# A retention layer and a gated feed-forward block on one core: next keys and queries prepared inside the group, activation table loaded early, w_in sums shared by VectorE and GpSimd

## The chip, the core and the metric

One core of a Trainium2 chip runs the whole kernel. The metric is the device time of one launch in microseconds. The kernel before takes 698.4 us (median of 3 runs, 698.11 to 699.78). q, k, v and the result are float32; the two weight matrices arrive as float64 and are made float32 in the kernel.

## The reference

A retention recurrence over 768 steps for 4 batches and 8 heads of 64 gives x, 3072 tokens of 512 features. A feed-forward block with 2048 hidden features follows, with the activation h * erf(softplus(h)).

```python
for t in range(S):
    state = gamma * state + einsum('bhd,bhe->bhde', k[:, :, t], v[:, :, t])
    y[:, :, t] = scale * einsum('bhd,bhde->bhe', q[:, :, t], state)
x = y.transpose(0, 2, 1, 3).reshape(3072, 512)
h = x @ w_in                       # w_in 512 x 2048
g = h * erf(softplus(h))
out = g @ w_out                    # w_out 2048 x 512
```

## The kernel before, in words

**Work items.** The recurrence is computed in 24 chunks j of 128 steps (6 for each batch). Each needs scaled keys and queries, their transposes, scores, a causal mask, products with the values, and an update of the state. The result lands transposed in xT, 512 tokens to a tile. The feed-forward block has a first stage and a second stage.

**First stage (g = 0 to 3).** The first 512 tokens go through plain matmuls. Group g covers 512 hidden features: `hidden` (L849 to L877) makes h, `gate_softplus` and `gate_erf` (L811, L824) apply the functions on ScalarE, `gated` (L843) multiplies by h on VectorE, and `project` (L879 to L899) multiplies by w_out one group later. In the same time the weights are brought from the 64-bit form in which they are stored to float32 by `conversion` (L285 to L336: L313, L317, L322, L325, L331 on VectorE, L314 on ScalarE). The conversions are steps of a generator; `pace(n)` emits n more of them and `need(...)` emits steps until a piece is done. `waiting` holds calls that `pace_around` runs in its middle.

**Second stage (g = 4 to 23).** The other 2560 tokens go in pairs of groups: a pair is one block of 256 tokens, its even group (g - 4 even) takes one half s = 0 of the hidden features, its odd group the half s = 1. Each group's first layer is computed by a bilinear scheme with 26 block products instead of 32. It needs sums of blocks of x (`x_sums`, 18 additions of 128x128, L931, once a pair) and sums of blocks of w_in (`sums_in(s)`, L338 to L343: 30 additions of 128x256 for each s, once in the kernel, on GpSimd). `hidden_steps` (L940 to L967) runs the 26 products (the table STEPS, L100): two matmuls each into one of four PSUM banks, after which ScalarE writes (L963, L965) or VectorE adds (L961) the bank into one or two of eight blocks of h. A later product that uses the same bank is added to what is there, so it has to wait until the bank has been read. The second layer is one with 7 block products instead of 8: it needs sums S1 to S4 of blocks of g (`g_sums`, L986) and T1 to T4 of blocks of w_out (`sums`, L345, L350: four additions of 128x1024 for each s, once in the kernel). `project_part(g, p)` (L1004) does product p; products 4, 5, 6, 7 use T4, T1, T2, T3.

**Order in a group g of the second stage (L1169 to L1228).** The order on every engine is the order in which the program emits instructions; nothing reorders them. A group emits the 26 steps, with products 1, 2, 4 of group g-1 after steps 14, 18 and 24, and with the S sums of g-1. Then come softplus (L811), `sub_visit(j, g)` (L707: TensorE's part of chunk j, and the scores of chunk j+1), in odd groups `x_sums` for the next pair, then `K_(j + 2)` and `T(j + 2)`, that is the scales (L509, L516 twice) and the two 32x32 block transposes (L531 twice) of the keys and queries of chunk j+2 on VectorE, the transfers of chunk j+3, erf (L824), products 5, 6, 7, 3 of group g-1, and `gated(g)` (L843 twice). In the first four groups a step of `last_steps` (the T sums) comes after projections (L1215, L1217, L1222). In g = 4 the projections of g = 3 are done: projection 0 after step 14 (L1187), 1 to 3 at the end (L1214).

**Around the change.** `sums_in(0)` is emitted in g = 3 (L1127) after `block_scales` (L472, which makes the scale table kq_b), `sums_in(1)` at the start of g = 4 (L1173). The keys and queries of chunk 6 and the x sums are emitted between the projections of g = 2 (L1157, L1160), the scores of chunk 6 at the start of g = 4 (L1174).

Of the kernel before, what the change touches and what calls it, by code (L numbers as in the profile page):

```python
# [12 lines left out]
F32 = mybir.dt.float32  # L13
# [6 lines left out]
P = 128  # L20
# [116 lines left out]
def kernel(  # L137
# [197 lines left out]
                done.update((which, 2 * i + u) for u in (range(2) if part is None else (part,)))  # L335
            yield  # L336

    def sums_in(s):  # L338

        assert all(("hidden", 2 * FG + s * FG + u) in done for u in range(FG))  # L340
        assert ("in", n_ft - 1) in done
        for to, a, b, sign in W_SUMS:
            nc.gpsimd.tensor_tensor(w_in_sb[:, s, to], w_in_sb[:, s, a], w_in_sb[:, s, b], op=OP[sign])  # L343

    def sums(s):  # L345

        assert ("project", s) in done
        x = {name: w_out_sb[:, s, at] for name, at in OUT.items()}
        for to, a, b in (("T1", "12", "11"), ("T2", "22", "T1"), ("T3", "22", "12"), ("T4", "21", "T2")):
            nc.vector.tensor_tensor(x[to], x[a], x[b], op=ALU.subtract)  # L350
            yield
        done.add(("sums out", s))

    done = set()

    def weights():


        pending = [conversion(n) for n in range(n_p)]
        begun = 0  # L360
        for n, steps in enumerate(pending):
            for k, _ in enumerate(steps, start=begun):
                yield
                if n > 4 and n + 1 < n_p and k == 2:
                    next(pending[n + 1])
                    yield
            begun = int(n > 4)

    def later_sums():
        for s in range(2):  # L370
# [132 lines left out]
    def ret_scale(j, i=None):  # L503

        if j >= NJ:
            return
        scaled.add(j)
        if j >= NB:
            nc.vector.tensor_tensor(  # L509
                KQ[j][:, 0], KQ[j][:, 0],  # L510
                kq_s[:, j % NC, 0, :, None].to_broadcast([P, H, D]), op=ALU.mult,
            )
            for i, x in enumerate((KB[j], KQ[j][:, 1].rearrange("p h d -> p (h d)"))):
                x = x.rearrange("p (u a d) -> p u a d", u=HP, d=32)
                by = kq_b[:, j % NC, i, :, :, None].to_broadcast([P, HP, 4, 32])
                nc.vector.tensor_tensor(x, x, by, op=ALU.mult)  # L516
            return
        part = slice(i, i + 1) if i is not None else slice(2)
        x = KQ[j][:, part]
        by = kq_s[:, j % NC, part, :, None].to_broadcast([P, x.shape[1], H, D])  # L520
        nc.vector.tensor_tensor(x, x, by, op=ALU.mult)
        pace(-1.1)

    def ret_transpose(j, part=None):
        assert j in scaled
        if j >= NB:
            for name, store, x in (
                ("k", KT, KB[j]), ("q", QT, KQ[j][:, 1].rearrange("p h d -> p (h d)"))
            ):
                store[j] = ret.tile([P, HP, C], F32, name=name + "T")  # L530
                nc.vector.transpose(store[j].rearrange("p u t -> p (u t)"), x)  # L531
            return
# [12 lines left out]
        pace(1)  # L545

    def ret_scores(j, pool=None):
        pp = SC[j] = [ret_psum(pool) for _ in range(2)]
# [455 lines left out]
    def project_part(g, p, at=slice(None)):  # L1004
        m, s = chunk_of(g), (g - G0) % 2
        if s == 0 and m not in O:
            O[m] = {}
            started.clear()
        a, b = PRODUCTS[p]
        if b[0] == "T":  # L1010
            need("sums out", s)
        i, half = (3, 1) if p == 4 and g >= NG - 2 else HOME[p]
        if i not in O[m]:
            O[m][i] = ps_o.tile([P, 2, DH], F32, name=f"o{i}")
        for u in range(FG):
            nc.tensor.matmul(  # L1016
                O[m][i][:, half, at],
                G[g][a][:, u * P : (u + 1) * P],
                w_out_sb[:, s, OUT[b], u, at],
                start=i not in started,  # L1020
                stop=(s == 1 and u == FG - 1),
                skip_group_check=True,
            )
            started.add(i)
        pace(1.5)
# [62 lines left out]
    def next_scores():  # L1088
# [35 lines left out]
        ],  # L1124
        [
            ([(load, 6), (sub_results, 5)], []),
            ([(load, 7), (block_scales,), (sums_in, 0)], [(sub_sums, 5)]),  # L1127
            ([], []),
            ([], []),
        ],  # L1130
    ]

    for g in range(G0):
        for u in range(FG):

            if g and u == (2 if g == 1 else 0):
                waiting.append((gated, g - 1))
            hidden(g, u)
            run(after[g][u][0])
            if (g, u) == (1, 0):  # L1140
                room = 0.0
            waiting.extend(after[g][u][1])
        gate(g)
        if g:
            for tt in range(TT):
                project(g - 1, tt)
                if g == 1 and tt < 2:
                    waiting.append((K_, 5) if tt else (sub_states, 4))
                elif g == 2 and tt == 0:
                    sub_results(4)  # L1150
                    sub_begin(5, ps_h)
                    load_block_scales()
                    waiting.append((sub_states, 5))
                elif g == 2 and tt == 2:
                    waiting.append((sub_sums, 4))
                elif g == G0 - 1 and tt == 0:
                    waiting.extend([(K_, JPC + 2), (T, JPC + 2)])  # L1157
                elif g == G0 - 1 and tt == 1:
                    load(JPC + 4)
                    waiting.append((x_sums, G0))  # L1160

    for _ in weight_steps:
        assert False, "weight steps left"

    j = JPC + 2
    put = None
    for g in range(G0, NG):  # L1169
        first = g == G0  # L1170
        more = j < NJ
        if first:
            sums_in(1)  # L1173
            sub_begin(j)  # L1174
            sub_states(j)
        elif put is not None:
            put_part(put, 0)
        more_sums = iter(()) if first else g_sums(g - 1)
        next(more_sums, None)
        for n, _ in enumerate(hidden_steps(g), start=1):  # L1180
            if first:
                if n in (5, 9):
                    gated(g - 1, n // 9)
                elif n == 14:
                    K_(j + 1)
                    T(j + 1)
                    project(g - 1, 0)  # L1187
                continue
            if put is not None and n in (14, 16, 18):
                put_part(put, n // 2 - 6)  # L1190
            for _ in range({14: 2, 18: 2}.get(n, 0) if put is None else {18: 1, 20: 1, 24: 2}.get(n, 0)):
                next(more_sums)
            if n in (14, 18, 24):
                project_part(g - 1, {14: 1, 18: 2, 24: 4}[n])
        put = None
        for _ in more_sums:
            pass

        gate_softplus(g)
        if more:  # L1200
            sub_visit(j, g)
        if g + 1 < NG and (g - G0) % 2:
            x_sums(g + 1)
        if more:
            if j + 2 < NJ:
                K_(j + 2)
                T(j + 2)
            if j + 3 < NJ:
                load(j + 3)
            j += 1  # L1210
        if first:
            gate_erf(g)
            for tt in range(1, TT):
                project(g - 1, tt)  # L1214
                next(last_steps)  # L1215
            put_first()
            next(last_steps)  # L1217
        else:
            gate_erf(g)
            for p in (5, 6, 7, 3):  # L1220
                project_part(g - 1, p)
                next(last_steps, None)  # L1222
            if (g - G0) % 2 == 0:
                put = chunk_of(g - 1)
        if g == NG - 1:
            last_gated(g)
        else:
            gated(g)  # L1228

    g, m = NG - 1, chunk_of(NG - 1)  # L1230
    for p, step in ((1, 0), (7, None), (2, None), (6, 1), (5, 2)):
# [56 lines left out]
```

## Time and profile before

| what | value |
|---|---|
| time, median of 3 | 698.4 us |
| span of the profiled execution | 697.9 us, granted TensorE clock 0.985 |
| first stage, to about 127.6 us | TensorE, VectorE nearly full; ScalarE about half |
| second stage, two groups | 53.9 us in most pairs |
| VectorE in two groups (244 to 298 us) | 39.7 us busy |
| GpSimd, w_in sums L343 | 60 instructions, 57.0 us busy, 113.5 to 172 us |
| ScalarE, table loads at L811 | 24 of 1283 ns |

Engines are PE (TensorE), PEld (its weight loads), DVE (VectorE), ACT (ScalarE), POOL (GpSimd) and SP (the queue that issues transfers). A line of a timeline gives start, length, engine, line of the program, operation, output <- inputs with shapes and a count; a bracket gives the idle time before it and what ended it. Idle time of an engine matters only where another engine, in the end TensorE, waits for it.

### The profile page before, as it was taken

Reading aid. Unit: us, or ns where it says so; the run is one execution under the profiler, and the core shown is the slowest. Engines: PE = TensorE matmul, PEld = TensorE weight load, DVE = VectorE, ACT = ScalarE, POOL = GpSimd, SP = SyncE. Lnnn points to the kernel's source line nnn. Section 1 sums busy time; section 2 is a strip of 40 time slices with the busy share of each in tenths; the row PEclk is TensorE's granted clock in tenths of the full one; section 3 lists DMA queues with packets and bytes.
Section 4 is the critical chain, followed back from the end, with each engine's and each line's share of the span. In section 5 each row is a group of like instructions: output and inputs, shape, how many; then the busy total and the mean of one; then the engine's idle time right before and its main releaser. Section 6 shows DMA issues by size and latency. Waiting matters only on the chain.

```text
span 697.9 us, 15334 instructions
## 1 busy us (share of the span) xinstructions
PE 665.0 (95%) x6240; PEld 565.4 (81%) x6240; DVE 521.4 (75%) x1067; ACT 267.8 (38%) x374; POOL 63.7 (9%) x80
## 2 busy tenths in 40 slices
PE   8999999799969989989989998998998998999998
PEld 7744444566969989989989998998998998999996
DVE  5999999889776786776775776777777577467364
ACT  3476545133414254153252451541541532424531
POOL 1000006998000000000000000000000000000000
PEclk9999999999989999999999999999999999999999
DMA  9999853333111222222321231231231220000000
GB/s 185 233 246 231 223 145 59 61 61 88 43 35 30 63 45 43 68 44 41 70 41 38 33 79 29 47 76 32 44 77 35 37 57 0 2 32 1 0 31 31
DMA packets 156726, 47.70 MB, mean 68 GB/s; under 512 B 143088, under 2 KB 147568, under 8 KB 156656
## 3 DMA queue, kind: packets, MB, share of 16 engines
q1 hardware_dynamic: 156240, 46.72, 30.5%
q8 instruction: 49, 0.80, 0.5%
q14 instruction: 21, 0.17, 0.1%
q10 hardware_dynamic: 416, 0.01, 0.0%
HBM read 40.39 MB, written 6.29 MB: 67 GB/s over the span
## 4 chain that ended last, share of the span: by engine, by line
PE 63%; DVE 20%; SPq 5%; issue 4%; ACT 4%; DMA 3%; DVEq 0%; ACTq 0%
PE o L1016 27%; PE hp L949 20%; PE r L949 10%; SPq L187 5%; DVE xs L931 4%; DVE e L843 2%; PE o L890 2%; DMA kq<-in_k_dram 2%; ACT e L811 1%; DVE h L961 1%; DVE w_out_sb L317 1%; DVE kb L516 1%; DVE kq L516 1%; DVE w_out_sb L325 1%; PE r L730 1%
## 5 line engine op out<-in xcount | busy, mean ns | idle before, releaser
L949 PE MATMUL hp<-xs,w_in_sb 128*128 128x128 f32 x1040 | 151.1, 282 | 21.8 <-DVE h L961 21.1
L949 PEld LDWEIGHTS hp<-xs,w_in_sb 128*128 128x128 f32 x1040 | 139.4, 197 | 27.5 <-DVE h L961 23.2
L1016 PE MATMUL o<-w_out_sb,h 128*128 128x256 f32 (+1 forms) x648 | 143.8, 379 | 0.4 <-DVE r L1243 0.4
L961 DVE TENSOR_TENSOR h<-h,hp 128x256 f32<-128x256 f32 x200 | 82.5, 420 | 74.6 <-PE hp L949 71.0
L1016 PEld LDWEIGHTS o<-w_out_sb,h 128*128 128x128 f32 x648 | 120.5, 190 | 17.1 <-DVE r L1243 0.6
L1016 PE MATMUL o<-w_out_sb,e 128*128 128x256 f32 x480 | 113.8, 380 | 0.0
L1016 PEld LDWEIGHTS o<-w_out_sb,e 128*128 128x128 f32 x480 | 87.0, 191 | 9.8 <-DVE e L977 0.4
L811 ACT ACT_TABLE_LOAD x24 | 30.8, 1283 | 153.0 <-DVE h L961 152.9
L961 DVE TENSOR_TENSOR h<-h,r 128x256 f32<-128x256 f32 x160 | 61.4, 418 | 22.9 <-PE r L949 19.2
L949 PE MATMUL r<-xs,w_in_sb 128*128 128x128 f32 x480 | 70.8, 287 | 4.9 <-DVE am L629 4.9
L949 PEld LDWEIGHTS r<-xs,w_in_sb 128*128 128x128 f32 x480 | 64.0, 203 | 5.1 <-issue 5.1
L963 ACT COPY h<-hp 128x256 f32<-128x256 f32 x40 | 14.9, 373 | 128.8 <-PE hp L949 92.6
L343 POOL TENSOR_TENSOR w_in_sb<-w_in_sb 128x256 f32<-128x256 f32 x60 | 57.0, 973 | 1.9
L843 DVE TENSOR_TENSOR e<-h,e 128x1024 f32<-128x1024 f32 x42 | 50.1, 1235 | 9.3 <-ACT e L824 9.3
L854 PE MATMUL hp<-xT,w_in_sb 128*128 128x512 f32 (+2 forms) x144 | 56.5, 548 | 0.0
L949 PE MATMUL hp<-xT,w_in_sb 128*128 128x128 f32 x320 | 48.9, 275 | 0.0
L854 PEld LDWEIGHTS hp<-xT,w_in_sb 128*128 128x128 f32 x144 | 25.7, 190 | 27.0 <-issue 24.6
L949 PEld LDWEIGHTS hp<-xT,w_in_sb 128*128 128x128 f32 x320 | 43.8, 192 | 1.5 <-issue 0.5
L965 ACT ACTIVATE h<-hp 128x256 f32<-128x256 f32 x60 | 23.1, 384 | 55.8 <-PE hp L949 54.4
L811 ACT ACTIVATE e<-h 128x2048 f32<-128x2048 f32 x22 | 42.0, 1911 | 5.3 <-DVE h L961 5.0
L824 ACT ACTIVATE e<-e 128x2048 f32<-128x2048 f32 (+1 forms) x23 | 42.1, 1836 | 0.2
L949 PE MATMUL r<-xT,w_in_sb 128*128 128x128 f32 x240 | 33.3, 275 | 0.0
(151 smaller groups left out, 780.1 us busy)
## 6 DMA issues: line engine op xcount, KB each, us to landing
w_out_sb<-in_moe_w_out_dram SPq DMA_DIRECT2D x14, 512.0 KB, 5.5
kq<-in_k_dram SPq DMA_DIRECT2D x23, 256.0 KB, 4.1
v<-in_v_dram SPq DMA_DIRECT2D x23, 256.0 KB, 3.1
out_dram<-r SPq DMA_DIRECT2D x23, 256.0 KB, 2.7
kq<-in_q_dram SPq DMA_DIRECT2D x288, 16.0 KB, 1.8
kb<-in_k_dram SPq DMA_DIRECT2D x288, 16.0 KB, 1.7
w_in_sb<-in_moe_w_in_dram SPq DMA_DIRECT2D x8, 512.0 KB, 11.3
w_in_sb<-in_moe_w_in_dram SPq DMA_DIRECT2D x8, 256.0 KB, 8.1
```

What stands on the lines that cost most here:

```text
L187: nc.sync.dma_start(to[part, u * C : (u + 1) * C].rearrange("p (a d) -> p a d", d=32), src[2 * u + s, :, d * 32 : (d + 1) * 32].rearrange( ...
L343: nc.gpsimd.tensor_tensor(w_in_sb[:, s, to], w_in_sb[:, s, a], w_in_sb[:, s, b], op=OP[sign])
L811: nc.scalar.activation(E[g], HS[g], AF.Softplus)
L824: nc.scalar.activation(E[g][:, half], E[g][:, half], AF.Erf)
L843: nc.vector.tensor_tensor(E[g][:, half], HS[g][:, half], E[g][:, half], op=ALU.mult)
L854: nc.tensor.matmul(HP_[ft][:, t], w_in_of(ft, kk), XC[0][:, kk, t], start=(kk == 0), stop=(kk == n_k - 1),)
L931: nc.vector.tensor_tensor(of(to), of(a), of(b), op=OP[sign])
L949: nc.tensor.matmul(to[:, u, :], w_in_sb[:, s, w, u * P : (u + 1) * P], XS[m](x), start=first and u == 0, stop=True, skip_group_check=True,)
L961: nc.vector.tensor_tensor(h, h, of, op=ALU.add if plus else ALU.subtract)
L963: nc.scalar.copy(h, of)
L965: nc.scalar.activation(h, of, AF.Copy, scale=-1.0)
L1016: nc.tensor.matmul(O[m][i][:, half, at], G[g][a][:, u * P : (u + 1) * P], w_out_sb[:, s, OUT[b], u, at], start=i not in started, stop=(s = ...
```

## The change

These things are changed. The five VectorE operations on the keys and queries are made a generator, `prepared(j)`; from g = 6 on, even groups emit those of chunk j+1 between their steps (10, 14, 16, 18, 24) and those of chunk j+2 where they were, and odd groups emit none; g = 4 and g = 5 each emit those of chunk j+1 between their steps. A small softplus on a spare tile is emitted ahead of each group's softplus, so that the table is loaded before h is complete. The w_in sums go to VectorE for s = 0 (16 after the piece ("out", 5) of the weights, 4 before g = 4, 10 in its first ten steps), and to GpSimd (20) and VectorE (10, behind erf of g = 4) for s = 1; a small GpSimd copy that reads the last sum of s = 0 stands ahead of GpSimd's twenty. Projections 0 and 1 of g = 3 ("two plain second-layer steps") are emitted ahead of the steps of g = 4, with gating, keys and queries, x sums and scores in between. The T sums are emitted in another order (T4 before T3) and at other places: two after the gating of g = 4, then after steps 1, 3 and 22 of g = 5 and 12 and 22 of g = 6, and the last one at the end of g = 6. The block scales are emitted two steps later.

The diff, cut to its core (the removed branches of `ret_scale` and `ret_transpose` for later chunks are the body of `prepared`):

```diff
-    def sums_in(s):
+    in_sums = [0, 0]
+    def sum_in(s, upto, engine=None):
-        for to, a, b, sign in W_SUMS:
-            nc.gpsimd.tensor_tensor(w_in_sb[:, s, to], w_in_sb[:, s, a], w_in_sb[:, s, b], op=OP[sign])
+        for to, a, b, sign in W_SUMS[in_sums[s] : upto]:
+            (engine or nc.vector).tensor_tensor(
+                w_in_sb[:, s, to], w_in_sb[:, s, a], w_in_sb[:, s, b], op=OP[sign]
+            )
+        in_sums[s] = max(in_sums[s], upto)
...
-        for to, a, b in (("T1", "12", "11"), ("T2", "22", "T1"), ("T3", "22", "12"), ("T4", "21", "T2")):
+        for to, a, b in (("T1", "12", "11"), ("T2", "22", "T1"), ("T4", "21", "T2"), ("T3", "22", "12")):
...
+            if pieces[n] == ("out", 5):
+                for k in range(4, 17, 4):
+                    sum_in(0, k)
+                    yield
...
+    def prepared(j):
+        if j >= NJ:
+            return
+        nc.vector.tensor_tensor(
+            KQ[j][:, 0], KQ[j][:, 0],
+            kq_s[:, j % NC, 0, :, None].to_broadcast([P, H, D]), op=ALU.mult,
+        )
+        yield
+        blocks = (KB[j], KQ[j][:, 1].rearrange("p h d -> p (h d)"))
+        for i, x in enumerate(blocks):
+            x = x.rearrange("p (u a d) -> p u a d", u=HP, d=32)
+            by = kq_b[:, j % NC, i, :, :, None].to_broadcast([P, HP, 4, 32])
+            nc.vector.tensor_tensor(x, x, by, op=ALU.mult)
+            yield
+        for name, store, x in zip("kq", (KT, QT), blocks):
+            store[j] = ret.tile([P, HP, C], F32, name=name + "T")
+            nc.vector.transpose(store[j].rearrange("p u t -> p (u t)"), x)
+            yield
...
-            ([(load, 7), (block_scales,), (sums_in, 0)], [(sub_sums, 5)]),
+            ([(load, 7)], [(sub_sums, 5)]),
             ([], []),
-            ([], []),
+            ([], [(block_scales,)]),
...
-                elif g == G0 - 1 and tt == 0:
-                    waiting.extend([(K_, JPC + 2), (T, JPC + 2)])
-                elif g == G0 - 1 and tt == 1:
-                    load(JPC + 4)
-                    waiting.append((x_sums, G0))
...
     j = JPC + 2
+    gated(G0 - 1)
+    all_of(prepared(j))
+    load(JPC + 4)
+    project(G0 - 1, 0)
+    x_sums(G0)
+    sub_begin(j)
+    project(G0 - 1, 1)
+    sub_states(j)
+    sum_in(0, 20)
...
+        next_chunk = prepared(j + 1) if even or put is None else iter(())
+        if put is not None:
+            order = {18: (e_sums,), 20: (e_sums,), 24: (e_sums, e_sums)}
+        else:
+            order = {
+                10: (next_chunk,), 14: (next_chunk, e_sums), 16: (next_chunk, e_sums),
+                18: (next_chunk, e_sums), 20: (e_sums,), 24: (next_chunk,),
+            }
+        if g == G0 + 1:
+            order.update({1: (last_steps,), 3: (last_steps,), 22: (last_steps,)})
+        elif g == G0 + 2:
+            order.update({12: (last_steps,), 22: (last_steps,)})
         for n, _ in enumerate(hidden_steps(g), start=1):
             if first:
+                sum_in(0, min(20 + n, len(W_SUMS)))
+                if n == 10:
+                    nc.gpsimd.tensor_copy(idle[:, :1], w_in_sb[:, 0, W_SUMS[-1][0], :1])
+                    sum_in(1, 20, nc.gpsimd)
...
+            for steps in order.get(n, ()):
+                next(steps, None)
...
+        nc.scalar.activation(idle[:, 1:], idle[:, 1:], AF.Softplus)
         gate_softplus(g)
         if more:
             sub_visit(j, g)
-        if g + 1 < NG and (g - G0) % 2:
+        if g + 1 < NG and not even:
             x_sums(g + 1)
         if more:
-            if j + 2 < NJ:
-                K_(j + 2)
-                T(j + 2)
+            if even and not first:
+                all_of(prepared(j + 2))
...
         if first:
-            gate_erf(g)
-            for tt in range(1, TT):
+            sum_in(1, len(W_SUMS))
+            for tt in range(2, TT):
                 project(g - 1, tt)
-                next(last_steps)
             put_first()
-            next(last_steps)
         else:
+            if g == G0 + 2:
+                all_of(last_steps)
             for p in (5, 6, 7, 3):
                 project_part(g - 1, p)
-                next(last_steps, None)
...
+        if first:
+            for _ in range(2):
+                next(last_steps)
```

More of the change, by code (lines that the diff above doesn't have):

```diff
@@ L336, in conversion @@
             yield
-    def sums_in(s):
+    in_sums = [0, 0]
+    def sum_in(s, upto, engine=None):
         assert all(("hidden", 2 * FG + s * FG + u) in done for u in range(FG))
-        assert ("in", n_ft - 1) in done
-        for to, a, b, sign in W_SUMS:
-            nc.gpsimd.tensor_tensor(w_in_sb[:, s, to], w_in_sb[:, s, a], w_in_sb[:, s, b], op=OP[sign])
+        for to, a, b, sign in W_SUMS[in_sums[s] : upto]:
[3 more added lines that the diff above has]
+        in_sums[s] = max(in_sums[s], upto)
     def sums(s):
@@ L348, in sums @@
         x = {name: w_out_sb[:, s, at] for name, at in OUT.items()}
-        for to, a, b in (("T1", "12", "11"), ("T2", "22", "T1"), ("T3", "22", "12"), ("T4", "21", "T2")):
+        for to, a, b in (("T1", "12", "11"), ("T2", "22", "T1"), ("T4", "21", "T2"), ("T3", "22", "12")):
             nc.vector.tensor_tensor(x[to], x[a], x[b], op=ALU.subtract)
+            done.add((to, s))
             yield
-        done.add(("sums out", s))
     done = set()
@@ L507, in ret_scale @@
         scaled.add(j)
[L508 to L517, printed above, removed]
         part = slice(i, i + 1) if i is not None else slice(2)
@@ L525, in ret_transpose @@
         assert j in scaled
[L526 to L532, printed above, removed]
         for i, (name, store) in enumerate((("k", KT), ("q", QT))):
@@ L1010, in project_part @@
         if b[0] == "T":
-            need("sums out", s)
+            assert (b, s) in done
         i, half = (3, 1) if p == 4 and g >= NG - 2 else HOME[p]
@@ L1155, with all_of @@
                     waiting.append((sub_sums, 4))
-                elif g == G0 - 1 and tt == 0:
-                    waiting.extend([(K_, JPC + 2), (T, JPC + 2)])
-                elif g == G0 - 1 and tt == 1:
-                    load(JPC + 4)
-                    waiting.append((x_sums, G0))
-    for _ in weight_steps:
-        assert False, "weight steps left"
-    j = JPC + 2
+    def all_of(steps):
+        for _ in steps:
+            pass
+    all_of(weight_steps)
+    idle = const.tile([P, 2], F32, name="idle_scalar")
@@ L1168 @@
+    nc.gpsimd.memset(idle, 1.0)
+    j = JPC + 2
+    gated(G0 - 1)
[7 more added lines that the diff above has]
+    sum_in(0, 20)
     put = None
     for g in range(G0, NG):
-        first = g == G0
+        first, even = g == G0, (g - G0) % 2 == 0
         more = j < NJ
[L1172 to L1176, printed above, removed]
-            put_part(put, 0)
@@ L1178 @@
-        more_sums = iter(()) if first else g_sums(g - 1)
-        next(more_sums, None)
+        if put is not None:
+            put_part(put, 0)
+        e_sums = iter(()) if first else g_sums(g - 1)
+        next(e_sums, None)
+        next_chunk = prepared(j + 1) if even or put is None else iter(())
+        if put is not None:
+            order = {18: (e_sums,), 20: (e_sums,), 24: (e_sums, e_sums)}
[4 more added lines that the diff above has]
+            }
@@ L1180 @@
+        if g == G0 + 1:
+            order.update({1: (last_steps,), 3: (last_steps,), 22: (last_steps,)})
+        elif g == G0 + 2:
+            order.update({12: (last_steps,), 22: (last_steps,)})
         for n, _ in enumerate(hidden_steps(g), start=1):
             if first:
[L1182 to L1188, printed above, removed]
+                sum_in(0, min(20 + n, len(W_SUMS)))
+                if n == 10:
+                    nc.gpsimd.tensor_copy(idle[:, :1], w_in_sb[:, 0, W_SUMS[-1][0], :1])
+                    sum_in(1, 20, nc.gpsimd)
@@ L1189 @@
             if put is not None and n in (14, 16, 18):
                 put_part(put, n // 2 - 6)
-            for _ in range({14: 2, 18: 2}.get(n, 0) if put is None else {18: 1, 20: 1, 24: 2}.get(n, 0)):
-                next(more_sums)
-            if n in (14, 18, 24):
+            for steps in order.get(n, ()):
+                next(steps, None)
+            if not first and n in (14, 18, 24):
                 project_part(g - 1, {14: 1, 18: 2, 24: 4}[n])
         put = None
-        for _ in more_sums:
-            pass
+        all_of(e_sums)
@@ L1199 @@
+        all_of(next_chunk)
+        nc.scalar.activation(idle[:, 1:], idle[:, 1:], AF.Softplus)
         gate_softplus(g)
@@ L1210 @@
             j += 1
+        gate_erf(g)
         if first:
-            gate_erf(g)
-            for tt in range(1, TT):
+            sum_in(1, len(W_SUMS))
+            for tt in range(2, TT):
                 project(g - 1, tt)
-                next(last_steps)
             put_first()
-            next(last_steps)
         else:
-            gate_erf(g)
+            if g == G0 + 2:
+                all_of(last_steps)
             for p in (5, 6, 7, 3):
                 project_part(g - 1, p)
-                next(last_steps, None)
-            if (g - G0) % 2 == 0:
+            if even:
                 put = chunk_of(g - 1)
```

## The prediction

> **What bounds the kernel now.** I read the page's parts 1 and 4 first, then the waits, then each engine's timeline around every idle stretch of TensorE. Busy time, shares of the chain, and two lines of the waits (waiter, releaser, us in total, times, longest):
>
> ```profile
> PE 665.0 (95%) x6240; PEld 565.4 (81%) x6240; DVE 521.4 (75%) x1067; ACT 267.8 (38%) x374; POOL 63.7 (9%) x80
> ...
> PE 63%; DVE 20%; SPq 5%; issue 4%; ACT 4%; DMA 3%; DVEq 0%; ACTq 0%
> ...
> PE hp L949 <- DVE h L961: 21.1, 11, 5.4
> PE r L949 <- DVE am L629: 4.9, 1, 4.9
> ```
>
> TensorE is the bound, and from 15 us to 134 us and inside most groups its timeline has no gap. So the change can win only the gaps and what follows them. TensorE's timeline shows them in brackets (start, length, what ran, idle before):
>
> ```profile
> 134.75 2.05 PE L949 MATMUL r<-xs,w_in_sb 128*128 128x128 f32 x8 [4.95 <-DVE am L629]
> ...
> 201.44 2.08 PE L949 MATMUL hp<-xs,w_in_sb 128*128 128x128 f32 x8 [5.41 <-DVE h L961]
> ...
> 257.67 1.16 PE L949 MATMUL hp<-xs,w_in_sb 128*128 128x128 f32 x8 [2.01 <-DVE h L961]
> ...
> 584.72 2.06 PE L949 MATMUL hp<-xs,w_in_sb 128*128 128x128 f32 x8 [2.00 <-DVE h L961]
> ```
>
> Seven stand at the ninth step of g=8, 10, ..., 20: 2.01, 1.81, 2.01, 2.01, 1.80, 2.01, 2.00, sum 13.65 us. Step 9 writes a PSUM bank that step 5 filled, so it waits until VectorE has read step 5. VectorE's timeline just before the gap of g=10 says why that read is late:
>
> ```profile
> 301.70 1.10 DVE L931 TENSOR_TENSOR xs<-xT 128x128 f32<-128x128 f32 x5
> ...
> 305.84 0.69 DVE L509 TENSOR_TENSOR kq<-kq,kq_s 128x512 f32<-128x512 f32 x1
> ...
> 308.86 2.32 DVE L843 TENSOR_TENSOR e<-h,e 128x1024 f32<-128x1024 f32 x2
> 311.10 0.42 DVE L961 TENSOR_TENSOR h<-h,hp 128x256 f32<-128x256 f32 x1
> ```
>
> The odd group ends with 18 x-sums (4.1 us), five operations on the next keys and queries (305.84 to 308.86, 3.0 us) and the gating (2.2 us). TensorE began g=10 at 306.03 and had the fifth step ready about 2.5 us later; the read came at 311.10.
>
> A gap also costs afterwards: the eight matmuls after 201.44 and 584.72 take 2.08 and 2.06 us instead of 1.16, as the granted clock falls (0.79 in 196 to 212 us). The distance between such gaps is 53.9 us, but 55.74, 55.75 and 56.23 where the clock fell: 1.86 us for a 2 us gap (3 of 7) and 2.3 us for the 5.4 us gap.
>
> **What the Trainium skill says.** "SBUF — State Buffer", section "SBUF: two separate sides": VectorE with two SBUF inputs and GpSimd reading SBUF exclude each other for a whole instruction. The trace agrees. While GpSimd does the w_in sums (113.5 to 172 us) the same operation takes 1.21 us that later takes 0.69, with no loss where an input is in PSUM (0.42 both times):
>
> ```profile
> 144.19 1.21 DVE L516 TENSOR_TENSOR kb<-kb,kq_b 128x512 f32<-128x512 f32 x1
> ...
> 306.44 0.69 DVE L516 TENSOR_TENSOR kb<-kb,kq_b 128x512 f32<-128x512 f32 x1
> ```
>
> "TensorE: Matmul & The Clock Gate", section "What's actually happening": the clock is halved after an idle window of some 3.4 us, and the window runs freely. That fits a cost of about 1.9 us which strikes only some 2 us gaps.
>
> **The change part by part.**
>
> *Keys and queries.* Odd groups lose the five operations. The gating of g=9 then ends at 311.1 - 3.0 = 308.1 or earlier, 0.4 us before step 5 of g=10 is ready: the gap closes. g=22, which has no keys left, already has none. The five go into even groups after steps 10, 14, 16, 18 and 24. I laid them between the reads of L961 with 0.60 us (scales), 0.63 (transposes), 0.33 (reads), from TensorE's start: a step is 0.446 us and a projection 1.73. The closest places are step 15, which needs the read of step 13 (done 7.1, needed 8.0), step 23 (12.6 against 13.3) and step 25 (14.9 against 15.9). All hold, so this adds nothing. Chunk j+2 stays at the end of even groups, where the read of step 5 had 1.28 us of slack (idle before 282.62). The transfers were issued two groups back. Gain: 13.65 + 3 x 1.86 = 19.2 us.
>
> *Table loaded early.* The 1.28 us load (L811, x24) follows 8 us of ScalarE idleness at every group, so the load and the small activation are hidden, and softplus, x-sums and gating come 1.28 us earlier. With the gaps closed nobody waits for that: zero, and at most the 0.4 us that weights waited for L977 in the last group.
>
> *Start of the second stage (127.6 us to the start of g=6 at 192.3).* Sixteen w_in sums on VectorE at 107 us: 128x256 interpolated between 0.20 us (128x128) and 0.60 (128x512) is 0.33, with some 0.12 for a dependent one: 6.4 us. Weights converted afterwards end at 123.5, erf of g=3 at 123.9 (ScalarE's L314 is queued behind), gating 126.2. TensorE wants it at 127.6: hidden by 1.4 us. Keys to 129.2, x-sums at uncontended speed (4.1 instead of 11.3 us) to 133.3. TensorE meanwhile has projection 0, scores, projection 1 until 135.5: the 4.95 us gap closes. The last 14 sums of s=0 lie among the reads of g=4 and end at 141.4; extra waits in g=4 are about 3 us; scores and projections 2, 3 end at 159.0, against 164.4 before.
>
> But g=5 needs the s=1 sums. GpSimd starts 20 at 141.7, at 0.72 to 0.77 us (its quiet pace: 16 to 17 in 11.5 us from 122 to 134 us, and a median of 768 ns), plus waits for VectorE: until 158.9 (up to 161.2 at its mean of 973 ns). Behind it on VectorE are queued the ten last sums, gating of g=4 (2.3 us) and four w_out sums (4.7 us) ahead of step 5's read: 161.3, 163.6, 168.3. TensorE, at step 9 by 163.4, waits until 168.7: a new gap of 5.3 us, and the clock falls (2 us). Before, step 9 of g=5 began at 169.85. From there to g=6 it is 22.45 us: 193.2 instead of 192.3, a loss of 0.9 us.
>
> *w_out sums moved.* Three stood before the gating of g=5 and made the 5.41 us gap; that and its 2.33 us of clock go: 7.7 us gained. They come back in g=6. T2 delays step 15 by 0.25 us. T4, after step 22, ends about 15.9 us into the group while product 4 could start at 14.4: 1.5 us. T3 stands behind the five operations at the end of g=6: where TensorE would reach product 7 about 3.5 us after the projections' start (at 276.6 in the timing of g=8), T3 would end near 278.95: 2.35 us. Sum 4.1, and with 3 in 7 for each of two gaps 1.6 us of clock: 5.7 us lost.
>
> *Sum:* 19.2 - 0.9 + 7.7 - 5.7 = 20.3 us: 698.4 - 20.3 = 678.1 us.
>
> **Rivals.** (1) *The wait moves into the even groups.* For it: VectorE was at work 20 of 27 us there and now reads PSUM in small pieces between 0.6 us blocks. Against: the free places counted above. At 1 us for 8 groups, with the clock falling in three, 8 + 5.6 = 14 us less: 692. At half of that, 685. (2) *The start goes better:* GpSimd at 0.72 us with no waits, gap under 3.4 us without a fall of clock, no clock loss in g=6: 20.3 + 2 + 2 + 1.6 = 26: 672; with the last group's 0.4 and no extra waits, 669. (3) *Slower:* if sixteen sums on a VectorE busy 39.45 of 40 us in 60 to 100 us reach the path (6.4 us), GpSimd's end comes 5 us later, and every even group stalls by 2 us with the clock falling each time (9 x 3.9 = 35): 698.4 - 20.3 + 6 + 5 + 35 = 724; with a fall in three of nine only, 713. Against: the sums come after all that TensorE needs before 127.6.
>
> **How the numbers follow.** Forecast (671 to 685) 0.70, rival 1 (685 to 695) 0.16, rival 2 (under 671) 0.07, rival 3 0.05, about no change 0.02. The range runs from 670 to 689: below it half of rival 2, above it half of rival 1 and the rest. Its unknown costs are GpSimd's pace (2.3 us), clock falls (2 each, up to three) and sums on VectorE (0.33 to 0.45 us each, 2 us). Chances: faster 0.92, same 0.03, slower 0.05.
>
> **What would show it.** No gap at step 9 of g=8 to 20 and 52 us for two groups instead of 53.9; no rise of waits inside even groups; one gap of 4 to 6 us in g=5, released by VectorE's first read of h there; in g=6 gaps of about 1.5 and 2.4 us at products 4 and 7, released by the w_out sums; the granted clock near 0.99. Wrong if even groups take over 26.2 us, if TensorE idles before 127 us, or if GpSimd's sums take over 1 us each.

## The result, and the profile after

The changed kernel takes 676.23 us (median of four executions, 675.23 to 677.14); the kernel before took 698.41 us (four, 698.11 to 699.78). The ratio is 0.9678 [0.9656, 0.9701]: 22.2 us, or 3.2%, faster. The prediction was 678.1. Single executions differ by some microseconds and by their granted clock, and the two that were profiled lie on opposite sides of their medians (before 699.63 us, after 675.38), so that spans read from the profiles differ by 24.6 us, more than the medians do.

The page after, parts 1 and 4 (busy time of each engine; shares of the chain that ended last), and from the waits the two largest that TensorE still has and one of VectorE (waiter, releaser, us in total, times, longest):

```profile
PE 657.0 (98%) x6240; PEld 558.1 (83%) x6240; DVE 519.7 (77%) x1107; ACT 272.1 (40%) x394; POOL 23.0 (3%) x42
...
PE 90%; DVE 5%; SPq 2%; DMA 1%; issue 1%; ACT 1%; DVEq 0%; ACTq 0%
...
PE hp L960 <- DVE h L972: 6.1, 3, 3.9
DVE xT L797 <- ACT xT L795: 4.8, 18, 1.4
PE o L1027 <- DVE w_out_sb L354: 3.4, 2, 2.2
```

The wait for VectorE's reads of h fell from 21.1 us in 11 places to 6.1 in 3. A new wait, for the w_out sums at L354, has 3.4 us. VectorE's wait for ScalarE's copies of xT was 26.5 us in as many places before; the experiments show which edit shortened it. VectorE did as much work as before (519.7 against 521.4 us), but on the chain its share fell from 20% to 5%.

The profiled executions split the gain in two. Before, TensorE was busy 665.0 of 697.9 us; after, 657.0 of 673.3. So 16.6 us are idle time that went (32.9 to 16.3), and 8.0 us are the same 6240 matmuls run at a higher granted clock (0.985 to 0.997).

Where this lies is told by the busy time of each engine in four stretches. In each line the stretch and its length are followed by TensorE's busy time, then PEld, VectorE, ScalarE and GpSimd, then the granted clock, the DMA share and GB/s. The kernel before:

```profile
127.00:193.00 66.00, 58.33 (x577) 47.33 (x576) 53.64 (x102) 21.64 (x34) 43.94 (x49) 0.97 0.31 65
193.00:245.00 52.00, 46.59 (x541) 43.96 (x539) 37.41 (x72) 14.64 (x25) 0.00 (x0) 0.93 0.20 42
245.00:349.00 104.00, 100.18 (x981) 93.56 (x982) 76.84 (x178) 38.81 (x58) 0.00 (x0) 1.00 0.25 52
349.00:660.00 311.00, 301.12 (x3148) 281.09 (x3148) 216.21 (x504) 118.25 (x168) 0.00 (x0) 0.98 0.18 37
```

The kernel after, the same stretches:

```profile
127.00:193.00 66.00, 59.10 (x581) 47.81 (x580) 58.55 (x136) 22.39 (x37) 16.14 (x21) 0.97 0.31 64
193.00:245.00 52.00, 48.56 (x555) 44.76 (x554) 38.62 (x87) 19.91 (x30) 0.00 (x0) 1.00 0.24 50
245.00:349.00 104.00, 104.00 (x1124) 97.41 (x1123) 78.92 (x185) 41.32 (x64) 0.00 (x0) 1.00 0.26 53
349.00:660.00 311.00, 310.95 (x3144) 291.00 (x3144) 223.94 (x514) 122.61 (x185) 0.00 (x0) 1.00 0.18 38
```

From 245 to 660 us TensorE has no gap and full clock. Between 127 and 193 us, where the sums were redistributed, it idles about as long as before (7.7 us before, 6.9 after). These are all its gaps after 125 us until the last group, from TensorE's timeline (start, length, what ran; in brackets the idle time before and what ended it):

```profile
143.81 0.71 PE L960 MATMUL hp<-xs,w_in_sb 128*128 128x128 f32 x4 [1.74 <-DVE h L972]
149.40 0.71 PE L960 MATMUL hp<-xs,w_in_sb 128*128 128x128 f32 x4 [0.51 <-DVE h L972]
161.91 0.68 PE L960 MATMUL hp<-xs,w_in_sb 128*128 128x128 f32 x4 [0.73 <-ACT h L974]
167.79 1.16 PE L960 MATMUL hp<-xs,w_in_sb 128*128 128x128 f32 x8 [3.85 <-DVE h L972]
207.77 1.99 PE L1027 MATMUL o<-w_out_sb,e 128*128 128x256 f32 x8 [1.20 <-DVE w_out_sb L354]
218.48 3.72 PE L1027 MATMUL o<-w_out_sb,h 128*128 128x256 f32 x16 [2.15 <-DVE w_out_sb L354]
```

The first two lie in g=4, where the last sums of s=0 stand among the reads. The third, early in g=5, was there before (0.73 us too). The fourth is the gap in g=5, the last two are those in g=6.

VectorE's timeline at the start of g=10 is the stretch in which the kernel before was late. It is now the reverse:

```profile
298.32 2.35 DVE L854 TENSOR_TENSOR e<-h,e 128x1024 f32<-128x1024 f32 x2
302.30 0.42 DVE L972 TENSOR_TENSOR h<-h,hp 128x256 f32<-128x256 f32 x1 [1.62 <-PE hp L960]
304.50 0.68 DVE L542 TENSOR_TENSOR kq<-kq,kq_s 128x512 f32<-128x512 f32 x1
307.09 0.68 DVE L551 TENSOR_TENSOR kb<-kb,kq_b 128x512 f32<-128x512 f32 x1
```

VectorE has done the gating and waits 1.62 us for TensorE's fifth step; the key operations come later, between steps. Two groups take 51.8 us from gating to gating (298.32 to 350.13), where 53.9 was the distance of the gaps before.

### The profile page after: what moved, and what is told of

Read it like the earlier page. It is cut to its first block, busy times and chain, and to the rows that moved or that the text cites. A ratio compares the mean times of both kernels' runs of the same rounds, so it can differ in the third digit from the quotient of the medians.

```text
span 673.3 us, 15344 instructions
## 1 busy us (share of the span) xinstructions
PE 657.0 (98%) x6240; PEld 558.1 (83%) x6240; DVE 519.7 (77%) x1107; ACT 272.1 (40%) x394; POOL 23.0 (3%) x42
## 4 chain that ended last, share of the span: by engine, by line
PE 90%; DVE 5%; SPq 2%; DMA 1%; issue 1%; ACT 1%; DVEq 0%; ACTq 0%
PE o L1027 35%; PE hp L960 21%; PE r L960 11%; PE hp L865 8%; PE o L901 7%; SPq L187 2%; PE r L741 1%; PE hp L633 1%; DVE w_in_sb L344 1%; PE o L777 1%; DVE h L972 1%; DVE w_out_sb L354 1%; DMA kq<-in_k_dram 1%; PE r L562 1%; PE o L609 1%
## 5 line engine op out<-in xcount | busy, mean ns | idle before, releaser
L960 PE MATMUL hp<-xs,w_in_sb 128*128 128x128 f32 x1040 | 147.0, 277 | 7.0 <-DVE h L972 6.1
L960 PEld LDWEIGHTS hp<-xs,w_in_sb 128*128 128x128 f32 x1040 | 135.7, 193 | 11.3 <-DVE h L972 7.4
L972 DVE TENSOR_TENSOR h<-h,r 128x256 f32<-128x256 f32 x160 | 59.9, 415 | 21.6 <-PE r L960 20.5
L960 PE MATMUL r<-xs,w_in_sb 128*128 128x128 f32 x480 | 67.1, 276 | 0.0
L960 PEld LDWEIGHTS r<-xs,w_in_sb 128*128 128x128 f32 x480 | 60.3, 193 | 0.0
L865 PEld LDWEIGHTS hp<-xT,w_in_sb 128*128 128x128 f32 x144 | 25.8, 190 | 27.0 <-issue 24.6
L835 ACT ACT_TABLE_LOAD x24 | 30.8, 1283 | 0.4
L960 PEld LDWEIGHTS r<-xT,w_in_sb 128*128 128x128 f32 x240 | 30.0, 192 | 0.0
```

Source lines behind the costliest of these rows:

```text
L835: nc.scalar.activation(E[g][:, half], E[g][:, half], AF.Erf)
L865: nc.tensor.matmul(HP_[ft][:, t], w_in_of(ft, kk), XC[0][:, kk, t], start=(kk == 0), stop=(kk == n_k - 1),)
L960: nc.tensor.matmul(to[:, u, :], w_in_sb[:, s, w, u * P : (u + 1) * P], XS[m](x), start=first and u == 0, stop=True, skip_group_check=True,)
L972: nc.vector.tensor_tensor(h, h, of, op=ALU.add if plus else ALU.subtract)
```

## The experiments

The theory: the keys and queries at the ends of odd groups cost nearly all that the change gains, through the seven gaps and the clock; the new start only exchanges one gap for others; the early table is hidden. The rivals: the gain comes from the table or from the redistributed sums, or the key operations would make even groups wait.

### One edit at a time on the kernel before

**Keys alone.** From g=7 on, the five operations leave the ends of odd groups and go into even groups.

```diff
+        inside = not first and (g - G0) % 2 == 0
+        next_chunk = prepared(j + 1) if inside and g > G0 + 2 else iter(())
         for n, _ in enumerate(hidden_steps(g), start=1):
+            if n in (10, 14, 16, 18, 24):
+                next(next_chunk, None)
...
-            if j + 2 < NJ:
+            if j + 2 < NJ and (g == G0 + 1 or (g - G0) % 2 == 0):
                 K_(j + 2)
                 T(j + 2)
```

> The kernel before with one edit: from g = 7 on the keys and queries leave the odd groups and go between the steps of the even groups. Theory of the prediction: the seven 2 us gaps at step 9 of g = 8 to 20 and three falls of the clock go, 13.65 + 5.6 = 19.2 us, so 679 us; the 5.41 us gap of g = 6 stays. Rival (the work only moves the wait into the even groups): gaps of about 1 us inside g = 8, 10, ..., 20 and no more than 6 us gained, 692 us or above.

680.14 us (679.96 to 681.05) against 699.33 (seven executions): ratio 0.9718 [0.969, 0.9746]. That is 19.2 us (17.8 to 21.7 by the interval), the size of the term in the prediction. No gap is left from g=8 to the last group, and the gaps at the start of g=4 (5.22 us) and in g=6 stay. TensorE's timeline of this kernel:

```profile
201.86 2.07 PE L969 MATMUL hp<-xs,w_in_sb 128*128 128x128 f32 x8 [5.41 <-DVE h L981]
```

**Table alone.** One small softplus ahead of `gate_softplus` in the kernel before.

```diff
+    idle2 = const.tile([P, 1], F32, name="idle_scalar")
+    nc.gpsimd.memset(idle2, 1.0)
...
+        nc.scalar.activation(idle2, idle2, AF.Softplus)
         gate_softplus(g)
```

> The kernel before with one edit: the small softplus ahead of each softplus. Theory (one chain, softplus - x sums - keys - gating, makes the gap, so anything cut out of it shortens it): the seven gaps fall from 2.0 to 0.7 us and the one of g = 6 from 5.41 to 4.1, with no fall of the clock after the seven: 8 x 1.28 + 5.6 = 15.8 us, so 682.6 us. Rival (the load is hidden in ScalarE's idle time and is worth nothing by itself, as it was costed in the prediction): 698.4 us.

684.96 us (684.62 to 685.06): ratio 0.9785 [0.9752, 0.9818], 14.4 us. Each of the eight gaps lost 1.28 us, the length of the load. Two of them in TensorE's timeline:

```profile
201.04 1.73 PE L949 MATMUL hp<-xs,w_in_sb 128*128 128x128 f32 x8 [4.12 <-DVE h L961]
...
308.12 1.16 PE L949 MATMUL hp<-xs,w_in_sb 128*128 128x128 f32 x8 [0.52 <-DVE h L961]
```

What were gaps of 1.8 to 2.0 us at step 9 of g=8 to 20 are now 0.72, 0.52, 0.73, 0.72, 0.52, 0.72, 0.72 (sum 4.65 instead of 13.65), and the clock falls after none of them. So 9.0 us of gaps, 1.3 in g=6 and three falls of 1.86 us are in it: 15.9 us, which the interval (12.7 to 17.3) takes in. The load was on the chain that makes the gaps. VectorE's timeline ahead of g=10, in the kernel before and in this one:

```profile
301.10 0.56 DVE L786 TENSOR_TENSOR xT<-xT,hp 128x128 f32<-128x128 f32 x2 [1.43 <-ACT xT L784]
```

```profile
297.65 0.56 DVE L786 TENSOR_TENSOR xT<-xT,hp 128x128 f32<-128x128 f32 x2 [0.16 <-ACT xT L784]
```

ScalarE does the load, the softplus and then the copy of xT for which this addition waits; behind the addition VectorE has the x sums, the five key operations, the gating and the read of step 5, and step 9 waits for that read. In all, VectorE waits 26.5 us for these copies in the kernel before, with the keys alone and in the changed kernel without the early table, and 4.8 us wherever the table is early. The Trainium skill ("ScalarE: Activation LUTs", section "What ACT_TABLE_LOAD costs") gives about 1283 ns for the load, which the traces show, and 1380 ns of drain with it; the gaps shrink by the 1.28 us alone.

### One edit taken out of the changed kernel

**No early table:** the line with the small softplus goes.

```diff
-        nc.scalar.activation(idle[:, 1:], idle[:, 1:], AF.Softplus)
         gate_softplus(g)
```

> The changed kernel without the small softplus that loads the table early. Theory of the prediction: in pairs from g = 8 on nothing waits for the 1.28 us, so no gap comes back; only where the T3 sum is the last to arrive (product 7 of g = 6, now a gap of 2.15 us) and in the last group does it show: 1.3 + 0.4 us, so 677.9 us. Rival (the early load carries part of the gain): 1.28 us for each of nine pairs, 11.5 us, so 688 us.

679.21 us (678.49 to 679.66): ratio 0.9701 [0.9673, 0.973]. Only one gap changed, the last one in g=6, from 2.15 to 3.43 us. TensorE's timeline:

```profile
220.84 4.33 PE L1027 MATMUL o<-w_out_sb,h 128*128 128x256 f32 x11 [3.43 <-DVE w_out_sb L354]
```

VectorE's timeline shows where it comes from:

```profile
215.76 0.56 DVE L797 TENSOR_TENSOR xT<-xT,hp 128x128 f32<-128x128 f32 x2 [1.43 <-ACT xT L795]
...
219.60 1.18 DVE L354 TENSOR_TENSOR w_out_sb<-w_out_sb 128x1024 f32<-128x1024 f32 x1
```

The addition to xT waits 1.43 us for ScalarE again (0.16 in the changed kernel), and the five key operations and T3, the sum at 219.60, stand behind it. The gap is 1.28 us longer, with a lower clock afterwards (0.992 over the span instead of 0.997). Once the keys have moved, the table is worth these 1.28 us and the clock: about 3 us by the medians, though the two ratios' intervals overlap.

**Keys back:** from g=5 on the five operations stand at the ends of groups, and the table stays early.

```diff
-        next_chunk = prepared(j + 1) if even or put is None else iter(())
+        next_chunk = prepared(j + 1) if g < G0 + 2 else iter(())
...
-            if even and not first:
+            if not first:
                 all_of(prepared(j + 2))
```

> The changed kernel with the keys and queries back at the ends of all groups from g = 5 on, the early table load kept. Theory (the early load and the move of the keys shorten the same chain): gaps of about 0.7 us come back at step 9 of g = 8 to 20, and one of about 1.6 us in g = 6, no fall of the clock; the T4 gap of g = 6 (1.2 us) goes as VectorE is freer there: 676.2 + 5 + 0.2 = 681.5 us. Rival (the two edits are separate, the keys carry 19 us by themselves): 695 us.

684.2 us (682.84 to 685.75): ratio 0.9774 [0.9739, 0.9809]. Gaps of 0.53 to 0.72 us are back at step 9 of g=6, 8 to 20. Two expectations missed. The gap of step 9 in g=6 was to be about 1.6 us and is 0.72. The gap of product 4 in g=6 was to go with the key operations, and stayed at 1.12 us. T4 is emitted after step 22, so VectorE takes it only after the read of that step; its place, not VectorE's load, makes it late.

**The new start alone:** both of the above edits together, so that only the sums, the start of the second stage and the places of the w_out sums differ from before.

> The changed kernel with both steady edits undone: no early table load, and from g = 5 on keys and queries at the end of every group. What is left is the new start of the second stage (shared w_in sums, two projections ahead, w_out sums moved). Theory of the prediction (that part only exchanges gaps): seven gaps of 2 us with three falls of the clock, in g = 6 one of 2.0 at step 9, 1.1 at product 4 and 3.4 at product 7, 3.85 in g = 5: 676.2 + 19.2 + 2.0 + 1.3 = 698.7 us, the time of before. Rival (the start carries a part of its own, the 4.95 and 5.41 us gaps that it closes): 692 us or less.

700.68 us (twelve executions, 699.62 to 702.44) against 701.32 (fifteen): ratio 1.0005 [0.9991, 1.002]. TensorE's timeline of g=6:

```profile
198.82 1.16 PE L960 MATMUL hp<-xs,w_in_sb 128*128 128x128 f32 x8 [2.01 <-DVE h L972]
211.06 1.99 PE L1027 MATMUL o<-w_out_sb,e 128*128 128x256 f32 x8 [1.13 <-DVE w_out_sb L354]
223.06 3.72 PE L1027 MATMUL o<-w_out_sb,h 128*128 128x256 f32 x16 [3.44 <-DVE w_out_sb L354]
```

The one gap of 5.41 us has become three of 6.58 together. The 4.95 us at the start of g=4 are gone, but step 9 of g=5 waits 3.84 us (0.77 before) and g=4 has 2.3 us inside it (1.23 before). By itself this third of the change is worth nothing that can be measured.

| edits in the kernel | ratio to before |
|---|---|
| start and w_out sums | 1.0005 [0.9991, 1.002] |
| table | 0.9785 [0.9752, 0.9818] |
| keys | 0.9718 [0.969, 0.9746] |
| start, table | 0.9774 [0.9739, 0.9809] |
| start, keys | 0.9701 [0.9673, 0.973] |
| all three | 0.9678 [0.9656, 0.9701] |

The table and the keys shorten the same chain: 2.15% and 2.8% alone, but no more than 3.2% together with the start. Table and keys without the start were not run, so what the start adds beside both of them is not measured.

### The w_in sums of s=0 on GpSimd

All thirty go back to GpSimd, at the piece of the weights where VectorE did sixteen.

```diff
             if pieces[n] == ("out", 5):
-                for k in range(4, 17, 4):
-                    sum_in(0, k)
-                    yield
+                sum_in(0, 30, nc.gpsimd)
```

> The changed kernel with the 30 w_in sums of s = 0 all on GpSimd, emitted at the place where VectorE now starts them; the s = 1 sums are shared as in the changed kernel. Theory (the ports of VectorE and GpSimd exclude each other): the x sums take about 11 us again instead of 4.1 and end near 140, so TensorE has a gap of about 4.5 us at the start of g = 4 with a fall of the clock, but the stalls in g = 4 (1.74 and 0.51) go, and as GpSimd's twenty sums still start near 141 the gap of g = 5 shrinks by what the start lost: 676 to 678 us. Rival (sharing the sums carries several us of its own): 682 us or more.

678.65 us (676.02 to 680.38) against 700.09 (seven): ratio 0.9708 [0.9681, 0.9735], which overlaps that of the changed kernel. GpSimd began at 92.5 us and was at work, with one break of 2.4 us for other operations, until 153 us. The expectation missed in part: the x sums were to take about 11 us and TensorE to wait 4.5 us at the start of g=4. VectorE's timeline of this kernel:

```profile
129.58 1.21 DVE L540 TENSOR_TENSOR kq<-kq,kq_s 128x512 f32<-128x512 f32 x1
...
136.88 2.37 DVE L940 TENSOR_TENSOR xs<-xT,xs 128x128 f32<-128x128 f32 x3
...
158.82 4.14 DVE L344 TENSOR_TENSOR w_in_sb<-w_in_sb 128x256 f32<-128x256 f32 x10
```

Beside GpSimd a key operation takes 1.21 instead of 0.68 us and the x sums end 7.4 us after they began (4.1 in the changed kernel), so TensorE waits 2.67 us for the transposed queries at 134.4 us. On the other hand GpSimd is done earlier, VectorE's last ten sums run alone in 4.14 us instead of 6.55, and the gap in g=5 is 1.44 instead of 3.85. What is won at one end is paid at the other. For these thirty sums the choice of the engine made no difference that can be measured; the run moves their engine and their time together, so it can't tell the two apart.

### The gaps that the change leaves

**w_out sums earlier in g=5 and g=6.** T2 of s=1 to the end of g=5, T4 to step 12 of g=6 and T3 ahead of the key operations.

```diff
         elif g == G0 + 2:
-            order.update({12: (last_steps,), 22: (last_steps,)})
+            order.update({12: (last_steps,)})
...
             x_sums(g + 1)
+        if g in (G0 + 1, G0 + 2):
+            next(last_steps)
```

> The changed kernel with three w_out sums of s = 1 moved: T2 to the end of g = 5 behind the x sums (1.42 us of slack there), T4 to step 12 of g = 6, T3 ahead of the five key operations at the end of g = 6. Theory of the prediction (the two gaps of g = 6, 1.20 and 2.15 us, come only from where the sums stand in VectorE's order): both go and nothing comes back, 676.2 - 3.35 = 672.9 us. Rival (VectorE has no room, the gaps come back at step 9 of g = 6 or of g = 7): 676 us.

671.64 us (671.57 to 672.38) against 701.32: ratio 0.9586 [0.9566, 0.9607]. Both gaps in g=6 are gone; that in g=5 is 3.84 as before.

**And fewer of them ahead of step 5 in g=5.** The two that stood after steps 1 and 3 of g=5 go after steps 12 and 22, and the rest move on by the same number of places.

```diff
         if g == G0 + 1:
-            order.update({1: (last_steps,), 3: (last_steps,), 22: (last_steps,)})
+            order.update({12: (last_steps,), 22: (last_steps,)})
         elif g == G0 + 2:
-            order.update({12: (last_steps,)})
+            order.update({5: (last_steps,), 12: (last_steps,)})
```

> As the run before, and in g = 5 only two w_out sums (T1, T2) stand ahead of the first read of h, T4 goes behind step 12 and T3 behind step 22; in g = 6 T2 goes behind step 5. Theory (the gap of g = 5 is VectorE's queue: GpSimd's sums, the last ten sums, gating, four w_out sums): the gap of 3.85 us falls by 2 x 1.15 to 1.55 us and the clock does not fall behind it (1.8 us): 672.9 - 4.1 = 668.8 us. Rival (the gap is set by GpSimd's sums alone): 672.9 us.

668.16 us (667.86 to 668.42): ratio 0.9533 [0.9509, 0.9557]. TensorE's timeline in g=5:

```profile
165.89 1.16 PE L960 MATMUL hp<-xs,w_in_sb 128*128 128x128 f32 x8 [1.45 <-DVE h L972]
```

The two sums took 2.4 us ahead of the read and the gap shrank by 2.4; the clock is at 1.000 over the span, and the time fell by 3.5 us.

**GpSimd makes fourteen of the s=1 sums, VectorE sixteen,** four of them behind the mask of the scores in g=4.

```diff
             sub_mask(j + 1)
+        if g == G0:
+            sum_in(1, 18)
...
-                    sum_in(1, 20, nc.gpsimd)
+                    sum_in(1, 14, nc.gpsimd)
```

> As the run before, and GpSimd takes 14 of the sums of s = 1 instead of 20, VectorE 16, of which four stand behind the mask of chunk 7, where VectorE waits for ScalarE. Theory (VectorE waits for GpSimd's last sums, 6.55 us for ten sums that take 3.6 alone): GpSimd ends 4 us earlier, VectorE has 6 more sums of 0.36 us, 1.4 of them in idle time, so the gap of g = 5 falls by another 1 to 1.5 us: 667.5 us. Rival (one sum costs as much wherever it stands): 668.8 us.

667.49 us (667.23 to 667.65): ratio 0.9524 [0.9505, 0.9544], the best of all: 4.8% under the kernel before, where the changed kernel is 3.2% under. The gap in g=5 fell only from 1.45 to 1.15 us; 1 to 1.5 us less was expected. Six sums fewer on GpSimd are six more on VectorE, which has the reads and the gating of the same stretch to do. The step from the version before is within both intervals.

## Why the prediction was right, point by point

**Keys and queries: right.** 19.2 us were predicted; alone they brought 19.2, and all seven gaps went. That the two agree to a tenth is luck, as the interval is 17.8 to 21.7. The reason holds in detail: VectorE was to be ready 0.4 us before step 5 of g=10; with the keys alone it waits 0.34 us there, and 1.62, the table's 1.28 more, in the changed kernel. No read in an even group came too late: TensorE is busy 104.00 of 104 us from 245 to 349 us. Rival 1 is out.

**The table: hidden from g=8 on, as predicted, but not worth zero.** "With the gaps closed nobody waits for that: zero" does not hold in g=6. T3 stands on VectorE behind the addition to xT, which waits for ScalarE, and TensorE waits for T3: without the early load its gap is 3.43 instead of 2.15 us. The prediction's own sum has this under another name. It puts T3's end at 278.95, while in the timing of g=8 that it uses the five key operations end at 279.02 and a sum takes about 1.2 us; the figure comes out only with the 1.28 us taken off. So the term was misnamed, and the total did not suffer. Zero is also no property of the edit. Alone it brings 14.4 us; the prediction booked the whole chain under the keys, which is one of two orders in which the sum can be told.

**Start of the second stage: right in mechanism, 1.3 us better than predicted.** g=6 starts at 191.88; 193.2 was predicted, 192.30 was before. The sixteen sums took 6.19 us (6.4 predicted) and reached nobody. The waits inside g=4 are 1.74 and 0.51 us, 1.0 us more than the 0.72 and 0.51 of before (about 3 more were predicted). The mis-sized term is the chain to step 9 of g=5. GpSimd's and VectorE's timelines:

```profile
142.11 16.29 POOL L344 TENSOR_TENSOR w_in_sb<-w_in_sb 128x256 f32<-128x256 f32 x20
```

```profile
153.79 6.55 DVE L344 TENSOR_TENSOR w_in_sb<-w_in_sb 128x256 f32<-128x256 f32 x10
160.26 2.35 DVE L854 TENSOR_TENSOR e<-h,e 128x1024 f32<-128x1024 f32 x2
162.53 4.87 DVE L354 TENSOR_TENSOR w_out_sb<-w_out_sb 128x1024 f32<-128x1024 f32 x4
167.32 0.41 DVE L972 TENSOR_TENSOR h<-h,hp 128x256 f32<-128x256 f32 x1
```

The order is the predicted one, about a microsecond sooner at each point: GpSimd's end at 158.4 (158.9), the ten sums' at 160.3 (161.3), the read at 167.3 (168.3). The gap is 3.85 instead of 5.3, a little under the 4 to 6 us named as the sign. The clock fell after it as predicted (0.91 granted from 160 to 180 us).

**w_out sums moved: right in place, 2.35 us too dear (5.7 predicted, 3.35 measured).** The gaps at products 4 and 7 are 1.20 and 2.15 us; 1.5 and 2.35 were predicted. The 0.25 us for T2 does not show. The clock term of 1.6 us did not come in the profiled execution: it was granted at 1.00 from 193 to 245 us.

**The sum: close in part by luck.** By the profiles: 19.2 for the keys, 0.4 for the start (192.30 to 191.88), 7.7 less 3.35 for the w_out sums, together 24.0, where the spans differ by 24.6 (697.9 and 673.3). Against the predicted 20.3 that is about 4 us more, 1.3 at the start and 2.35 in g=6 of it. The medians differ by 22.2 only, for two reasons of about equal size. The prediction read its gaps and falls of the clock in an execution of 699.63 us, 1.2 us above the median from which it subtracted them. And the changed kernel's executions are two and two: 675.38 and 675.23 us with a clock of 0.997, 677.14 and 677.08 with 0.994 and 0.995, so the profiled one lies 0.85 us under their median. The 1.8 us between the pairs are the size of one fall of the clock; which gap brings it stays open. So the terms that were predicted too low and these 2.1 us cancel in part, and the median came out 1.9 us under the prediction.

**Rival 2** would have had no clock loss in g=5 and 669 to 672 us; it needed a gap under 3.4 us there, and 3.85 came. One part of it came true: no clock loss in g=6, in the profiled execution. **Rival 3** failed at its first step: nothing before 127 us is longer (TensorE busy 112.00 of 112 us from 15 us on in both kernels).

## What to carry to other kernels

Ask of a gap which instructions stand on the chain to the late read, on all engines: two edits that shorten the same chain (here a table load on ScalarE and five operations on VectorE) do not add up, and each is worth most when it is made first. An engine that is busy 75% of the time can still be late at one place, so the useful question is in which order it takes its work: the operations moved here cost VectorE the same time wherever they stood. When sums are moved off one deadline, list the next deadlines too: the larger gaps that the change left came from its sums' new places, and reordering the w_out sums alone gave another 8 us (668.16 us against 676.23, ratios to before 0.9533 and 0.9678).

## What the runs showed that was not expected

**A short gap may cost nothing more than itself.** The Trainium skill ("TensorE: Matmul & The Clock Gate", section "What's actually happening") has an idle window of about 3.4 us that runs freely. In the profiles, no gap of 0.5 to 1.75 us was followed by a fall, nor was the one of 2.15 in the changed kernel. Of the seven gaps of about 2 us of the kernel before, three were, by one of 1.86 us; those of 3.84 us and more that are shown or named here all were. Between them it goes both ways: the 3.43 us without the early table and the 2.67 with the sums on GpSimd were followed by a fall (0.66 granted in the next 5 us each time), the 3.44 us of the new start alone by none. So 1.28 us off each of seven gaps was worth some 1.9 us each in the kernel with the table alone (14.4 us less the 1.3 of g=6, over seven). Why a gap shorter than the window can do it at all, and only sometimes, no run here shows. The prediction took it that the freely running window picks the gaps; that stays its reading.

**VectorE and GpSimd slow each other more where operations are small.** The skill ("SBUF — State Buffer", section "SBUF: two separate sides") says that one of them excludes the other for a whole instruction. The same three x sums of 128x128 took 2.37 us beside GpSimd's sums and 0.82 in the changed kernel, where GpSimd was idle. That is 0.8 us each, about the length of one GpSimd sum (0.73 us at the median in the changed kernel), so they may have taken turns; no view shows that. The 128x512 operations went from 0.68 to 1.21, less than twice. GpSimd's own sums had a median of 1.11 us over all fifty of the kernel with the s=0 sums on GpSimd. A read with an input in PSUM kept 0.41 to 0.42 us.
